# The first load as two halves of 64 partitions, one issued by SyncE and one by ScalarE

## The chip, the core and the metric

The kernel runs on one core of a Trainium2 chip. A core has TensorE (PE; its weight loads are listed apart as PEld), VectorE (DVE), ScalarE (ACT), GpSimd (POOL) and SyncE (SP), and 16 DMA engines that move data between HBM and the on-chip buffer (SBUF, 128 partitions). DMAs are issued by an engine's instruction into that engine's queue: SyncE's is q1 in the profile, ScalarE's is q10. The metric is the device time of one execution in microseconds; a profiled execution also gives a trace, whose span runs from the first to the last instruction.

## The reference

One token attends to two cached attention blocks, A with 16 heads and B with 16 query heads over 8 key heads. The two results are mixed by a gate.

```python
q = (x @ wq).reshape(B, Sq, H, Dh).transpose(0, 2, 1, 3)          # 448 -> 16 x 256
p = softmax(einsum("bhqd,bhkd->bhqk", q, k_cache) * Dh ** -0.5)   # over 8192 keys
a = einsum("bhqk,bhkd->bhqd", p, v_cache) -> (1, 1, 4096) @ wo    # the same for b, with k, v
                                                                  # repeated for two heads each
g = sigmoid((x * gate_w).sum(-1, keepdims=True))
return g * a + (1 - g) * b
```

Keys and values of A (16 heads) and of B (8 heads) are 8192 x 256 float32 each: 24 heads x 2 x 8.39 MB. With the weights, 432 MB are read once and 448 numbers are written.

## The kernel before

All inputs are laid out ahead of time as one long array, `stream`, in the order in which the kernel wants them. `plan()` (line 42) lists the pieces: the token and gate weights ("xg"), the query weights of a step ("wq"), tiles of keys ("k") and of values ("v", three tiles behind their keys), the output weights ("wo"). There are 8 steps; each has three units of work (a pair of B's heads that share keys, and two heads of A), each unit four tiles of 2048 keys. The pieces are packed into loads of up to `FULL` = 15872 floats per partition (62 KB, 7936 KB over 128 partitions). The first load holds 15368 floats per partition: "xg", the first "wq", two tiles of keys and most of a third.

The loads go into a ring of three buffers of SBUF, the tile named `slot`. The loop at line 629 walks over the list: it takes the next buffer, issues the load with `nc.sync.dma_start` on SyncE's queue, and then calls `piece()` for every piece in it, which issues the work on it. `Recorder.call` (line 147) tracks which instruction reads or writes what, and puts a wait on a semaphore where an engine or a DMA has to wait for another; every DMA has a semaphore of its own (dma0, dma1, ...). The instructions all appear at line 183 of the profile, where the recorder issues them, so tiles tell them apart. A load into a buffer waits until all that read its former content is done. So SyncE issues three loads at once at the start, and each later one when its buffer comes free.

On the first load, VectorE copies the token into `xz` (function `inputs`), TensorE multiplies it with the query weights (`project`), ScalarE and TensorE turn and spread the query (`spread`), and then the scores of the first keys follow: TensorE multiplies into `ps_sc`, VectorE takes minima (`mn`), ScalarE the exponential (`px`), VectorE turns it (`pr`). For one unit per step ("by row") VectorE multiplies the keys in the buffer itself and sums (`slot<-slot,qa`, `sr<-slot`). Values are multiplied on TensorE into `ps_o`. ScalarE issues one DMA in the whole kernel, at its end: half of the output. SyncE issues the other half.

```python
    for fill in LOADS:
        buf = ring.tile([P, FULL], F32, name="slot")
        c = 0
        for load in fill:
            n = sum(x[3] for x in load)
            nc.sync.dma_start(buf[:, c:c + n], stream[off:off + P * n].rearrange("(p n) -> p n", p=P))
```

Of the kernel before, what the change touches and what calls it, by code (L numbers as in the profile page):

```python
# [9 lines left out]
P = 128  # L10
# [214 lines left out]
def program(nc, stream, out):  # L225
    nc.alloc_sbuf_tensor("pad", [P, -((nc.sbuf_base + 31) // 32 * 32) % 256 // 4 or 64], F32)
    memory = {("slot", i): nc.alloc_sbuf_tensor(f"slot_{i}", [P, FULL], F32) for i in range(SLOTS)}
    plan = Recorder(nc, memory)
    build(plan, stream, out)
    names = ["tensor", "vector", "scalar", "gpsimd"] + plan.dmas  # L230
    sems = {n: nc.alloc_semaphore(f"{n[0]}{n[1]}" if n[0] == "dma" else n) for n in names}
    rec = Recorder(nc, memory, plan.needed | {(e, plan.count[e] - 1) for e in names[:4]}, sems)
    stores = build(rec, stream, out)
    late = rec.wait("sync", [(e, rec.count[e] - 1) for e in names[:4]] + [d for d in rec.dmas if d not in stores[1:]])
    for sem, value in late:
        nc.sync.wait_ge(sem, value)
    nc.sync.sem_clear(range(sems[names[0]].num, sems[stores[1]].num))
    for d in stores[1:]:
        nc.sync.wait_ge(sems[d], 16)
    nc.sync.sem_clear(range(sems[stores[1]].num, sems[stores[-1]].num + 1))  # L240


def build(nc, stream, out):
# [335 lines left out]
    def piece(kind, i, at, view):  # L579
        n = view.shape[-1] // ATOM[kind]  # L580
        j0 = at // ATOM[kind]
        if kind == "xg":
            inputs(view[:, :KF + 1])
            GW[0] = view[:, KF + 1:]
        elif kind == "wq":
            project(i, j0, view.rearrange("p (c n) -> p c n", c=n))
            if j0 + n < 2 * KF + 1:
                pass
            elif i == 0:
                spread(0)  # L590
                prepare(GW[0])
            else:
                wait(1, spread, i)
        elif kind == "k":
            u, t = TILES[i]
            if u in BY_ROW:
                scores_by_row(u, t, 2 * j0, view.rearrange("p (j d) -> p j d", d=DH))
            else:
                scores(u, t, j0, view.rearrange("p (c n) -> p c n", c=n))
            if j0 + n < 2 * NG:  # L600
                return
            tick()
            if t == NT - 1:
                gather(u)
                wait(1, combine, u)
                wait(2, column, u)
        elif kind == "v":
            u, t = TILES[i]
            n = view.shape[-1] // DH
            attend(u, t, at // DH, n, view.rearrange("p (j d) -> p j d", d=DH))  # L610
            if at // DH + n == ROWS:
                if t == NT - 1:
                    take(u)
                    if u != TILES[-1][0]:
                        wait(1, project_o, u)
                if i >= len(TILES) - LEAD:
                    tick()
        elif kind == "half":
            emit_half(i, view)
        elif kind == "wo" and i < NS - 1:  # L620
            emit_set(i, j0, view.rearrange("p (c n) -> p c n", c=n))
            if i == NS - 2 and j0 + n == 8:
                fold()
        else:
            for j in range(n):
                LAST[divmod(j0 + j, 2)] = view[:, j * D:(j + 1) * D]

    off = 0
    for fill in LOADS:
        buf = ring.tile([P, FULL], F32, name="slot")  # L630
        c = 0
        for load in fill:
            n = sum(x[3] for x in load)
            nc.sync.dma_start(buf[:, c:c + n], stream[off:off + P * n].rearrange("(p n) -> p n", p=P))
            off += P * n
            for x in load:
                piece(*x[:3], buf[:, c:c + x[3]])
                c += x[3]
# [71 lines left out]
```

## Time and profile before

| | |
|---|---|
| median of 3 runs | 1007.69 us (1007.64 to 1007.72) |
| profiled execution | 1007.64 us |
| its span | 1006.0 us |
| mean granted TensorE clock | 0.771 |
| read from HBM | 432.02 MB |
| loads by SyncE | 64, of which 50 of 7936 KB and the first of 7684 KB |

The page gives busy time by engine, the span in 40 slices (25.15 us each), the DMA queues, the chain of work that ended last, and groups of instructions with the idle time ahead of them and what ended it. The issue rows of the trace give the time from issue to landing of a DMA. The table of windows gives, for any stretch, each engine's busy time and the packets that the DMA engines started in it, as a share of 16 engines and in GB/s; in stretches shorter than a packet the share can exceed 1, since a packet counts in full where it starts. Queues called "instruction" (q8, q14) fetch program code.

### The profile page before, as it was taken

How to read it: one execution, taken by the hardware profiler on the slowest of the kernel's cores; microseconds unless marked ns; L12 is line 12 of the kernel's file. 1: busy time of each engine (PE TensorE's matmuls, PEld its weight loads, DVE VectorE, ACT ScalarE, POOL GpSimd, SP SyncE). 2: the span in 40 equal slices, each digit the busy share in tenths (PEclk: the TensorE clock that was granted, in tenths of full speed). 3: DMA queues.
4: the chain of work that ended last, by engine and by line, in shares of the span. 5: the costliest groups of instructions: out<-in, count | busy, mean ns of one | idle time of the engine just before them, and what ended most of it. 6: DMA issues, size and time to landing. Idle time of an engine off the chain costs nothing.

```text
span 1006.0 us, 7381 instructions
## 1 busy us (share of the span) xinstructions
PE 577.4 (57%) x3154; PEld 168.9 (17%) x3154; DVE 458.5 (46%) x642; ACT 94.5 (9%) x308; POOL 1.9 (0%) x10
## 2 busy tenths in 40 slices
PE   1846746654645665646736565545555647536557
PEld 0212211121111111112211121111111112111112
DVE  1386213961248521566214851248521585115951
ACT  0100100010100110001100011100110101101011
POOL 0000000000000000000000000000000000000000
PEclk9977787777786787787877777776777877777779
DMA  9999999999999999999999999999999999999997
GB/s 394 443 442 432 420 440 440 434 422 437 440 432 429 430 442 432 432 432 440 428 434 435 439 423 435 442 435 422 435 442 437 422 432 442 438 427 425 442 419 332
DMA packets 9256, 432.48 MB, mean 430 GB/s; under 512 B 1032, under 2 KB 1288, under 8 KB 1928
## 3 DMA queue, kind: packets, MB, share of 16 engines
q1 hardware_dynamic: 9220, 432.02, 99.3%
q8 instruction: 24, 0.39, 0.1%
q14 instruction: 8, 0.07, 0.0%
q10 hardware_dynamic: 4, 0.00, 0.0%
HBM read 432.02 MB, written 0.00 MB: 429 GB/s over the span
## 4 chain that ended last, share of the span: by engine, by line
DMA 75%; DVE 12%; PE 11%; ACT 1%; issue 0%; SPq 0%
DMA slot<-in_stream_dram 75%; PE ps_o L183 5%; DVE sr L183 5%; DVE slot L183 5%; PE ps_sc L183 5%; PE ps_s L183 1%; DVE pr L183 1%; DVE mn L183 1%; ACT px L183 1%; ACT ew L183 0%; ACT pxr L183 0%; DVE st L183 0%; PE ps_y L183 0%; DVE wr L183 0%; DVE mt L183 0%
## 5 line engine op out<-in xcount | busy, mean ns | idle before, releaser
L183 PE MATMUL ps_o<-slot,pr 128*32 128x512 f32 (+1 forms) x1536 | 346.6, 752 | 241.3 <-DMA slot<-in_stream_dram 241.1
L183 PE MATMUL ps_sc<-slot,qb 128*32 128x512 f32 x1024 | 194.4, 713 | 97.9 <-DMA slot<-in_stream_dram 97.8
L183 DVE TENSOR_REDUCE mn<-ps_sc 128x1 f32<-128x512 f32 x64 | 44.1, 689 | 310.4 <-PE ps_sc L183 281.9
L183 DVE TENSOR_TENSOR slot<-slot,qa 128x4096 f32<-128x4096 f32 (+7 forms) x39 | 142.4, 3652 | 45.5 <-DMA slot<-in_stream_dram 45.5
L183 PEld LDWEIGHTS ps_o<-slot,pr 128*32 128x32 f32 (+1 forms) x1536 | 79.1, 141 | 421.0 <-DMA slot<-in_stream_dram 272.5
L183 DVE TENSOR_REDUCE sr<-slot 128x16 f32<-128x4096 f32 (+7 forms) x39 | 142.5, 3654 | 1.3
L183 PEld LDWEIGHTS ps_sc<-slot,qb 128*32 128x32 f32 x1024 | 46.2, 129 | 215.7 <-DMA slot<-in_stream_dram 113.1
L183 ACT ACTIVATE px<-ps_sc,st 128x512 f32<-128x512 f32 x64 | 44.0, 688 | 377.7 <-DVE st L183 377.7
L183 DVE STREAM_TRANSPOSE pr<-px 128x512 f32<-128x512 f32 x64 | 45.7, 714 | 54.2 <-ACT px L183 54.2
L183 PE MATMUL ps_s<-slot,xz 128*32 128x512 f32 (+1 forms) x136 | 46.3, 656 | 36.2 <-DVE xz L183 22.1
L183 ACT ACTIVATE pxr<-sr,st 128x16 f32<-128x16 f32 x32 | 9.9, 308 | 376.5 <-DVE st L183 376.5
L183 DVE SCALAR_TENSOR_TENSOR ob<-ps_o,half,ob 128x256 f32<-128x256 f32 x24 | 11.4, 475 | 69.3 <-ACT ob L183 69.3
L183 PE MATMUL ps_s<-sel,ob 128*128 128x1 f32 (+1 forms) x96 | 17.0, 281 | 25.1 <-DVE ob L183 25.1
L183 PEld LDWEIGHTS ps_s<-sel,ob 128*128 128x128 f32 x96 | 15.0, 221 | 48.4 <-DVE ob L183 42.2
L183 PEld LDWEIGHTS ps_s<-slot,xz 128*32 128x32 f32 (+1 forms) x136 | 11.6, 122 | 66.6 <-issue 28.6
L183 DVE TENSOR_TENSOR pr<-pxr,cols 128x256 f32<-128x256 f32 x32 | 13.6, 425 | 15.0 <-ACT pxr L183 15.0
L183 ACT ACTIVATE ob<-ps_o,half 128x256 f32<-128x256 f32 x24 | 11.3, 471 | 67.0 <-PE ps_o L183 66.9
L183 PE MATMUL ps_y<-slot,ocs 128*1 128x448 f32 (+1 forms) x176 | 16.7, 497 | 0.0
L183 PE MATMUL ps_s<-ones,wr 1*128 1x1 f32 x48 | 9.9, 273 | 11.6 <-DVE wr L183 11.6
L183 PE MATMUL ps_s<-px,spread 64*128 64x256 f32 x16 | 7.2, 537 | 12.7 <-DVE es L183 12.7
L183 PEld LDWEIGHTS ps_s<-ones,wr 1*128 1x128 f32 x48 | 7.8, 204 | 34.5 <-DVE wr L183 20.2
L183 ACT ACTIVATION_READ_ACCUMULATOR px<-ps_sc,st 128x1 f32 x64 | 12.4, 193 | 0.0
(62 smaller groups left out, 138.9 us busy)
## 6 DMA issues: line engine op xcount, KB each, us to landing
slot<-in_stream_dram SPq DMA_DIRECT2D x50, 7936.0 KB, 42.1
slot<-in_stream_dram SPq DMA_DIRECT2D x1, 7684.0 KB, 21.1
slot<-in_stream_dram SPq DMA_DIRECT2D x1, 4608.0 KB, 40.2
slot<-in_stream_dram SPq DMA_DIRECT2D x2, 2048.0 KB, 33.9
slot<-in_stream_dram SPq DMA_DIRECT2D x1, 3328.0 KB, 38.4
slot<-in_stream_dram SPq DMA_DIRECT2D x1, 1536.0 KB, 32.2
slot<-in_stream_dram SPq DMA_DIRECT2D x3, 448.0 KB, 33.3
slot<-in_stream_dram SPq DMA_DIRECT2D x1, 1024.0 KB, 32.6
```

What stands on the lines that cost most here:

```text
L183: i = getattr(e, what)(*args, **kw)
```

## The change

Only the load at the start of `stream` (`off == 0`) differs. Its rows are divided: partitions 0 to 63 are loaded by a DMA of SyncE, partitions 64 to 127 by a DMA of ScalarE, into the same columns of the same buffer. All other loads stay on SyncE's queue.

```diff
             n = sum(x[3] for x in load)
-            nc.sync.dma_start(buf[:, c:c + n], stream[off:off + P * n].rearrange("(p n) -> p n", p=P))
+            rows = stream[off:off + P * n].rearrange("(p n) -> p n", p=P)
+            if off == 0:
+                nc.sync.dma_start(buf[:P // 2, c:c + n], rows[:P // 2])
+                nc.scalar.dma_start(buf[P // 2:, c:c + n], rows[P // 2:])
+            else:
+                nc.sync.dma_start(buf[:, c:c + n], rows)
             off += P * n
```

On ScalarE, at the start of the program, these are the first instructions before (`px`, `qa` and `ge` belong to the query and the gate, `px,st` to the exponentials of the first scores):

```order
L183 ACT_TABLE_LOAD
L183 ACTIVATE px<-ps_s 64x512
L183 ACTIVATE qa<-ps_s 128x256
L183 ACTIVATE ge<-ps_s 1x1
L183 ACTIVATE px,st<-ps_sc,st 128x512 x4
L183 ACTIVATE pxr,st<-sr,st 128x16
```

and these with the change:

```order
L183 DMA slot<-in_stream_dram 64x15368
L183 ACT_TABLE_LOAD
L183 ACTIVATE px<-ps_s 64x512
L183 ACTIVATE qa<-ps_s 128x256
L183 ACTIVATE ge<-ps_s 1x1
L183 ACTIVATE px,st<-ps_sc,st 128x512 x4
```

The issue of the second half stands first on ScalarE, ahead of the load of its function table; the rest keeps its order. On VectorE, a piece of the difference at the place where the token is first read (`xz` is its tile; the names in brackets are the semaphores waited for):

```order
 L183 MEMSET qb_0 128x128 x4
 L183 MEMSET xz 128x160
-L183 COPY xz<-slot 128x3 [waits dma0,vector]
+L183 COPY xz<-slot 128x3 [waits dma0,dma1,vector]
 L183 COPY xz<-slot 64x1 x2
 L183 TENSOR_SCALAR qb_0<-ps_s 128x2x2 [waits tensor]
```

The copy waits for both halves. The loads after the first have numbers one higher, and on SyncE the first row covers 64 partitions instead of 128; nothing else moves on any engine.

## The prediction

> **What bounds the kernel now.** I read the page's first three parts, then the chain of waits, then SyncE's own waits, then the table of windows over the start.
>
> ```profile
> span 1006.0 us, 7381 instructions
> PE 577.4 (57%) x3154; PEld 168.9 (17%) x3154; DVE 458.5 (46%) x642; ACT 94.5 (9%) x308; POOL 1.9 (0%) x10
> DMA  9999999999999999999999999999999999999997
> GB/s 394 443 442 432 420 440 440 434 422 437 440 432 429 430 442 432 432 432 440 428 434 435 439 423 435 442 435 422 435 442 437 422 432 442 438 427 425 442 419 332
> q1 hardware_dynamic: 9220, 432.02, 99.3%
> q10 hardware_dynamic: 4, 0.00, 0.0%
> DMA 75%; DVE 12%; PE 11%; ACT 1%; issue 0%; SPq 0%
> ```
>
> No engine is busy more than 57% of the span, while packets of queue q1 (SyncE's loads) fill 99.3% of what 16 DMA engines could do. The rate is flat from the second slice to the last but one. The chain calls 75% DMA; its DVE and PE parts are the work that frees a buffer before the next load is issued. Whether that ever starves the queue is seen here:
>
> ```profile
> DMA to landing us min/median/max: 21.1/40.6/58.7
> slot<-in_stream_dram SPq DMA_DIRECT2D x1, 7684.0 KB, 21.1
> slot<-in_stream_dram SPq DMA_DIRECT2D x2, 7936.0 KB, 49.0
> 0.74 0.39 SPq L183
> 1.20 39.29 DMA slot<-in_stream_dram
> 1.65 0.43 SPq L183 DMA_DIRECT2D slot<-in_stream_dram  x1
> 37.12 0.33 SPq L183 DMA_DIRECT2D slot<-in_stream_dram  x1
> 21.90 0.40 DVE L183 COPY xz<-slot 128x3 f32<-128x3 f32 x3 [15.88 <-DMA slot<-in_stream_dram]
> ```
>
> A full load is 128 x 15872 x 4 bytes = 8.13 MB, 18.9 us at 430 GB/s. The median load lands 40.6 us after its issue, more than two such times: when one is issued, over a load is still ahead of it in the ring. So the kernel is one stream of 432 MB that never runs dry, and the end comes when the stream ends. An edit at the start is worth exactly what it does to the stream's bytes per microsecond there. That the first data come earlier or later to the engines costs nothing by itself. The first load is issued at 0.74 and lands at 21.84 us (VectorE uses it at 21.90). The fourth load, which reuses its buffer, is issued at 37.12, 15.3 us after that landing. The second, issued at 1.20, lands 39.29 us later; with a mean of 49.0 for the two 7936 KB loads of the start, the third, issued at 1.65, lands 58.7 us later, the longest of all, at about 60.3, so 23 us of stream stand ahead of the fourth. The first load may land up to 23 us later, with the others in place, before the ring empties.
>
> **The start, packet by packet.** The columns are window, length, busy time of PE, PEld, DVE, ACT and POOL, granted clock, DMA share, GB/s. A packet is counted where it starts, so share x 16 x length / count is the mean time of one.
>
> ```profile
> 1.70:1.80 0.10, 0.00 (x0) 0.00 (x0) 0.10 (x2) 0.10 (x1) 0.10 (x1) 1.00 6.09 1844
> 2.40:2.50 0.10, 0.00 (x0) 0.00 (x0) 0.07 (x2) 0.00 (x0) 0.00 (x0) 1.00 1.98 615
> 2.50:2.60 0.10, 0.00 (x0) 0.00 (x0) 0.10 (x2) 0.00 (x0) 0.00 (x0) 1.00 0.00 0
> 4.90:5.00 0.10, 0.00 (x0) 0.00 (x0) 0.04 (x1) 0.00 (x0) 0.00 (x0) 1.00 5.67 2459
> 253.00:253.10 0.10, 0.10 (x5) 0.09 (x9) 0.10 (x1) 0.00 (x0) 0.00 (x0) 1.00 1.46 635
> ```
>
> One row of the first load is 15368 x 4 = 61,472 bytes, and 1844 GB/s x 0.1 us is three of them: one packet is one partition's row, 128 packets in all, 8 for each of 16 engines. All 16 engines start between 1.7 and 2.5 us, and nothing starts in the next window. The first packets take 6.09 x 16 x 0.1 / 3 = 3.25 us. In the second round four packets take 5.67 x 16 x 0.1 / 4 = **2.27 us** each: 27.1 GB/s per engine. In mid-kernel a 63,488-byte row takes 1.46 x 16 x 0.1 = 2.34 us, again 27.1. Sixteen times 27.1 is 434, the flat rate of the page. So each packet moves at a fixed 27.1 GB/s, and the engines start their rounds in step.
>
> **The change, part by part.** SyncE's half and ScalarE's half carry the same 7.87 MB as before, 64 packets each, 4 per engine, if each half is spread over 16 engines as every load here is.
>
> *Issue.* ScalarE gets one issue ahead of its table load.
>
> ```profile
> 0.73 1.28 ACT L183 ACT_TABLE_LOAD   x1 [0.73 <-PEq L697]
> 28.77 0.59 ACT L183 ACTIVATE px<-ps_s 64x512 f32<-64x512 f32 x1 [26.75 <-PE ps_s L183]
> 1003.77 1.10 ACTq L183 DMA_DIRECT2D out_dram<-ys  x1
> ```
>
> The only issue of ScalarE in the trace took 1.10 us, so the table load slips by about that, to end near 3.1 us; ScalarE's first work was at 28.77, behind 26.75 us of idle time. Cost 0; the idle time covers it. SyncE's issue stays first in its queue. VectorE's first COPY waits for two semaphores where it waited for one, and those queued behind it on VectorE (the query's setup, then the first score reductions) come with it; priced by the 23 us of slack above: 0.
>
> *The two rings on one engine.* New is that each of the 16 engines has packets of two queues at once. The nearest rows are the instruction fetches (q8, q14) that meet the loads. Ahead of each row stands the window in which the packet starts, then the queue's packets, MB and share of 16 engines.
>
> ```profile
> 254.80:254.90 0.10, 0.10 (x8) 0.09 (x4) 0.10 (x1) 0.00 (x0) 0.00 (x0) 1.00 3.48 1434
> q8 instruction: 1, 0.02, 110.1%
> 255.70:255.80 0.10, 0.10 (x8) 0.05 (x4) 0.00 (x0) 0.00 (x0) 0.00 (x0) 1.00 1.81 635
> q1 hardware_dynamic: 1, 0.06, 361.5%
> ```
>
> The q8 packet starts at 254.85 and takes 110.1% x 16 x 0.05 us = 0.88 us; a load packet starts at 255.75, just as it ends, and takes 361.5% x 16 x 0.05 = 2.89 us where 2.34 is usual. So an engine changes queue between packets, not inside one, and the load's packet behind a change is 0.55 us longer. For the first load that is up to 8 such changes on each engine: between 0 (both rings have their packets ready) and 8 x 0.55 = 4.4 us.
>
> *Where the packets of a round go.* Before, the 16 packets of a round are spread over the 128 rows of the buffer. Now the engines, in step, take a round from SyncE's ring and then one from ScalarE's. All 16 packets of a round lie in partitions 0-63, and of the next in 64-127. Whether the 27.1 GB/s is what an engine can move, or what the stretch of buffer it writes can take, no row tells, since no load of this kernel covers less than 128 partitions. If it is the engine, a round still takes 2.27 us: 0. If it is the destination, twice as many engines share each and a round takes 4.54 us: 8 x 2.27 = **+18.2 us** on the first load. Two engines that share a destination and started apart by d each have it alone for d in every round. The starts spread over 0 to 0.7 us; I take 0.3, which gives back 8 x 0.3 = 2.4. [...]
>
> [...]
>
> *Sum.* I take the destination: 18.2 - 2.4 = +15.8 us. The profiled execution took 1007.64 (span 1006.0 and 1.64 around it), 0.05 under the median of 1007.69. Forecast 1007.64 + 15.8 = **1023.4 us**. Bounds of this case: 18.2 - 8 x 0.7 = +12.6 (1020.2) and 18.2 + 4.4 = +22.6 (1030.2). None of it is won back later, since the ring behind it is never dry: the first load would land near 37.6, the fourth be issued 15.3 us later at 53, and the third, shifted as well, land near 76.
>
> **The rivals.**
> - *Queue changes alone.* The engine is the limit, but each alternation costs what the fetch rows show. 7 changes x 0.55 = 3.9 us gives 1011.5; between half and all eight of them, 1009.8 to 1012.0. For: measured here on load packets. Against: a fetch comes alone and unannounced, while ScalarE's ring has its four packets ready beside SyncE's.
> - *No change: the same 16 engines, the same bytes.* It decides if 27.1 GB/s is the engine's and a waiting ring is ready at once: every packet still 2.27 us, 1007.6, with at most the 0.9 us by which the first packets exceed the second, either way: 1006.7 to 1008.6. For: nothing in the trace moves slower when more or fewer packets start together. Against: the 0.55 us row. [...]
> - *Faster.* Two issuers would fill 16 engines sooner. The whole stretch from the first issue at 0.74 to the last engine's start at 2.5 is 1.8 us, under 0.2% (2.0 us, about what a measurement of this kernel can tell from no change).
> - *The change doesn't do what it says.* The order of instructions shows ScalarE's issue first on its engine, ahead of the table load, with the same release as SyncE's. If its half came a packet late it would land 2.27 us later among the second load's packets, at the same total: the no-change case.
>
> **How the numbers follow.** Engine or destination is open by the trace, so I give each half. The destination reading needs the engines in step as well, and the starts show that: **0.50** for the forecast. The other half splits between queue changes alone (**0.25**), no change (**0.23**) and faster (**0.02**). Slower by over 0.2% are the first two, less a sliver where only few changes cost: 0.74; within 0.2%: 0.24; faster 0.02. The forecast's own range is 1020.2 to 1030.2. To leave out no more than 2 in 10 the range must take in the no-change case too: 1007.2 to 1027.5, which leaves out the top of the forecast's own range, where all eight queue changes would cost in full, and the bottom of the no-change case.
>
> **What would show it.** In the changed profile queue q10 should hold some 64 large packets, 3.9 MB. Forecast: packets of both queues in the first 38 us take about 4.2 to 4.5 us, the first slice of GB/s falls from 394 to some 200 to 250, VectorE's COPY starts near 37 and the fourth issue comes near 53; from there all rows read as before, some 16 us later. Queue changes alone: packets of 2.8 us, COPY near 26. No change: packets of 2.27 us, COPY at 22. I am wrong if the first load's packets keep 2.27 us, or if lost time at the start is won back by the end, which would mean that the stream was not the bound.

## The result and the profile after

The changed kernel takes 1025.89 us (median; 1025.82 to 1026.13), beside 1007.72 us (1007.64 to 1007.91) for the kernel before in the same series: a ratio of 1.018 (1.0169 to 1.0191), 18.2 us slower. One run of the first try with two loads, further down, fell in a slower state (1066.94 us) and is left out of the figures there. From the page of the changed kernel, the span, the DMA slices (25.6 us each) and the queues:

```profile
span 1024.5 us, 7382 instructions
DMA  9999999999999999999999999999999999999998
GB/s 223 310 425 429 432 434 434 434 431 434 435 434 434 436 432 434 434 436 434 434 432 429 434 432 434 434 435 436 434 434 436 432 431 434 435 436 432 436 410 335
q1 hardware_dynamic: 9156, 428.09, 97.5%
q10 hardware_dynamic: 84, 3.94, 1.8%
DMA 73%; PE 13%; DVE 11%; ACT 1%; issue 0%; another core or an unknown queue 0%; SPq 0%; DVEq 0%
```

Nearly the whole loss is in the first two slices: 223 and 310 GB/s where before stood 394 and 443; from the third on (425 and up) the rate is about the old one. The DMA share stays at nine tenths or more all the while. The DMA engines are not idle at the start; their packets take longer. The timeline gives the issues and the first use of the load:

```profile
0.74 0.61 ACTq L183 DMA_DIRECT2D slot<-in_stream_dram  x1
1.37 1.28 ACT L183 ACT_TABLE_LOAD   x1 [1.37 <-PEq L702]
41.18 0.40 DVE L183 COPY xz<-slot 128x3 f32<-128x3 f32 x3 [35.17 <-DMA slot<-in_stream_dram]
56.47 0.33 SPq L183 DMA_DIRECT2D slot<-in_stream_dram  x1
```

VectorE's first COPY moved from 21.90 to 41.18 us, and the fourth load's issue follows 15.3 us later, as before. The DMA queues in the windows 6 to 7 us (first line) and 11 to 12 us (second), with packets, MB and their time as a share of 16 engines:

```profile
q10 hardware_dynamic: 11, 0.68, 317.0%
q1 hardware_dynamic: 12, 0.74, 345.5%
```

A packet of ScalarE's half takes 317.0% x 16 us / 11 = 4.61 us, one of SyncE's half 345.5% x 16 / 12 = 4.61 us, instead of 2.27. Between 2.0 and 40 us there are eight rounds of 16 packets, and the windows show the queues taking turns. 8 x (4.61 - 2.27) = 18.7 us stands beside a difference of the spans of 18.5. That close an agreement is partly chance. The first round took 4.45 us, and before it had taken 3.1 and not 2.27, so the eight rounds are worth 1.35 + 7 x 2.34 = 17.7 us. The rest is a start that came 0.4 us later and a first round of the second load that took 2.8 us instead of 2.35.

### The profile page after: what moved, and what is told of

The parts are those of the page before. It is cut to its first block, busy times and chain, and to the rows that moved or that the text cites. A ratio compares the mean times of both kernels' runs of the same rounds, so it can differ in the third digit from the quotient of the medians.

```text
span 1024.5 us, 7382 instructions
## 1 busy us (share of the span) xinstructions
PE 576.6 (56%) x3154; PEld 169.0 (17%) x3154; DVE 458.9 (45%) x642; ACT 94.4 (9%) x308; POOL 1.9 (0%) x10
## 4 chain that ended last, share of the span: by engine, by line
DMA 73%; PE 13%; DVE 11%; ACT 1%; issue 0%; another core or an unknown queue 0%; SPq 0%; DVEq 0%
DMA slot<-in_stream_dram 73%; PE ps_o L183 6%; PE ps_sc L183 5%; DVE sr L183 4%; DVE slot L183 4%; PE ps_s L183 2%; DVE pr L183 1%; ACT px L183 1%; DVE mn L183 1%; PE ps_y L183 0%; ACT ew L183 0%; DVE st L183 0%; DVE wr L183 0%; ACT pxr L183 0%
## 5 line engine op out<-in xcount | busy, mean ns | idle before, releaser
L183 PE MATMUL ps_sc<-slot,qb 128*32 128x512 f32 x1024 | 198.0, 728 | 95.0 <-DMA slot<-in_stream_dram 94.9
L183 PE MATMUL ps_s<-sel,ob 128*128 128x1 f32 (+1 forms) x96 | 16.7, 278 | 26.7 <-DVE ob L183 26.7
L183 PE MATMUL ps_y<-slot,ocs 128*1 128x448 f32 (+1 forms) x176 | 14.6, 447 | 0.0
L183 PEld LDWEIGHTS ps_s<-ones,wr 1*128 1x128 f32 x48 | 7.4, 193 | 30.9 <-DVE wr L183 17.7
```

The source lines that it names most:

```text
L183: i = getattr(e, what)(*args, **kw)
```

## The experiments

All differ from the changed kernel in the issue of the first one or two loads only; of each diff the lines that say how are shown. The packets that a queue has for one DMA engine are called its ring there. D is the theory that the written part of the buffer sets the rate, Q that two rings on an engine cost the time, L that the late landing of the first load does.

**Both halves on SyncE.**

```diff
-                nc.scalar.dma_start(buf[P // 2:, c:c + n], rows[P // 2:])
+                nc.sync.dma_start(buf[P // 2:, c:c + n], rows[P // 2:])
```

> Both 64-partition halves of the first load are issued by SyncE, one behind the other; ScalarE issues none. Theory D (the part of the buffer that a round of packets goes to is the limit: in a round all 16 packets lie in one half, so each takes twice as long): packets of the first load 4.5 to 4.6 us again, VectorE's first COPY near 41, 1025 to 1027 us. Rival Q (two rings on one engine cost the time): packets of 2.27 us, COPY near 22, 1007.5 to 1008.5 us.

Measured: 1027.24 us, ratio 1.0193 (1.0177 to 1.0208). Queue q1 from 6 to 7 us:

```profile
q1 hardware_dynamic: 12, 0.74, 361.2%
```

That is 4.82 us a packet, with no second ring, a little above the 4.5 to 4.6 that was expected (as the time is above 1025 to 1027). ScalarE's part in the change is not what costs; Q falls.

**Two queues, all partitions each.**

```diff
+                nc.sync.dma_start(buf[:, c:c + n // 2], rows[:, :n // 2])
+                nc.scalar.dma_start(buf[:, c + n // 2:c + n], rows[:, n // 2:])
```

> The first load is divided by columns, not by partitions: SyncE and ScalarE each load half of the columns of all 128 partitions. Theory D: rows of 30.7 KB, 16 packets per engine at 1.13 us, 18.2 us for the load as before, 1007.5 to 1008.5 us. Rival Q: a change of queue at every packet; with the 0.55 us that a load packet took longer behind a fetch, 16 x 0.55 = 8.8 us, 1016 us; with the doubling of the changed kernel, 1026 us.

Measured: 1007.54 us, ratio 0.9997 (0.9988 to 1.0007). The queues from 9 to 10 us:

```profile
q1 hardware_dynamic: 14, 0.43, 99.7%
q10 hardware_dynamic: 2, 0.06, 14.2%
```

Rows of 30.7 KB take 99.7% x 16 / 14 = 1.14 us, 27 GB/s for each engine, though the queues take turns: from 10 to 11 us 13 packets of q10 start beside 2 of q1. The changes between the two rings cost nothing here that can be measured (1007.54 us beside 1007.67 for the kernel before in the same series); the 0.55 us behind an instruction fetch does not carry over to them.

**Smaller neighbourhoods**, all on SyncE: four DMAs of 32 partitions, and eight of 16.

```diff
+                for q in range(0, P, 32):
+                    nc.sync.dma_start(buf[q:q + 32, c:c + n], rows[q:q + 32])
```

> Four DMAs of 32 partitions each (0-31, 32-63, 64-95, 96-127), all by SyncE. Theory D leaves open how partitions share destinations. If evenly by neighbourhood, a quarter has a quarter of the rate: packets of 9.1 us, 8 x (9.1 - 2.27) = +54.6 us, 1062 us. If a quarter reaches as much as the half it lies in: 4.6 us, 1026 us. Rival Q: 1007.7 us. [...]

> Eight DMAs of 16 partitions each, all by SyncE, one packet per engine and DMA. Theory D: packets at least twice as long as those of the run with 32 partitions if 16 partitions reach half as much as 32: 9.1 us and 1062 us if those took 4.6; 18.2 us and 8 x (18.2 - 2.27) = +127 us, 1135 us, if those took 9.1. If 16 reach as much as 32, the time of that run again. Rival Q: 1007.7 us.

Measured: 1026.97 us (ratio 1.0189, 1.0172 to 1.0206) with 32 partitions and 1058.45 us (1.0502, 1.0481 to 1.0523) with 16. Queue q1 with 32 partitions, from 6 to 7 us:

```profile
q1 hardware_dynamic: 12, 0.74, 361.4%
```

and with 16, from 36 to 37 us, where ten of the 20 packets are rows of 61 KB and ten are of under 512 B:

```profile
q1 hardware_dynamic: 20, 0.61, 550.1%
```

Seven packets of under 512 B take 0.8% x 16 / 7 = 0.02 us each in the run with 8 rows out of step below (queue q1, 14 to 15 us), so a row takes (550.1% x 16 - 10 x 0.02) / 10 = 8.8 us with 16 partitions. It is 4.82 us with 32, just as with 64. So DMAs into 32 neighbours moved as fast as into 64, and those into 16 little more than half as fast. With 32 that is the case that was put at 4.6 us and 1026, with 16 the one at 9.1 us and 1062.

**Even and odd partitions.**

```diff
+                nc.sync.dma_start(buf[0::2, c:c + n], rows[0::2])
+                nc.scalar.dma_start(buf[1::2, c:c + n], rows[1::2])
```

> Again 64 rows for SyncE and 64 for ScalarE, but the even partitions for one and the odd ones for the other, so that each half covers the whole buffer. If what counts is how much of the buffer a half reaches: packets of 2.3 us, 1007.5 to 1008.5 us. If any 64-row DMA loses half the rate, or rows that share a destination still meet in a round: 4.6 us, 1026 us. If ScalarE's part in it matters: 1026 us too.

Measured: 1007.87 us, ratio 1.0002 (0.9992 to 1.0011). `Recorder.call` takes the two interleaved halves for overlapping and makes ScalarE's wait, so it was issued only at 13.4 us, after SyncE's had landed. SyncE's half alone, from 9 to 10 us:

```profile
q1 hardware_dynamic: 10, 0.61, 141.8%
```

2.27 us a packet: 64 rows at full rate, with no other half beside them. Neither the number of rows nor the missing partner is the cost; that the rows are neighbours is (4.61 us a packet in the changed kernel).

**Which side of the transfer.** The two loads are issued as four halves, the first spread where it is written and together where it is read, the second the other way round (`second` is the second load's part of the stream, `early[1]` its buffer).

```diff
+                nc.sync.dma_start(buf[0::2, c:c + n], rows[:P // 2])
+                nc.sync.dma_start(early[1][:P // 2, :m], second[0::2])
+                nc.scalar.dma_start(buf[1::2, c:c + n], rows[P // 2:])
+                nc.scalar.dma_start(early[1][P // 2:, :m], second[1::2])
```

> One side of the transfer at a time. The first load's halves are read as rows 0-63 and 64-127 of the stream, but written to the even and the odd partitions. The second load's halves are read as even and odd rows, but written to partitions 0-63 and 64-127. So both loads put their rows into other partitions than the reference wants. If the written side sets the rate (theory D): packets of the first load 2.27 us, of the second 4.6 to 4.8 us. If the side that is read sets it: the first 4.6, the second 2.34. If neither alone does: all near 2.3, 1008 to 1010 us; if each does: all 4.6 to 4.8, 1043 to 1046 us. Total for either side alone: 1024 to 1029 us.

Measured: 1035.13 us (two runs, 1032.81 and 1037.45). As in the run before, ScalarE's issues waited, until 13.27 us. The queues from 9 to 10 us (the first load's even half), from 16 to 17 us (the second load's first half) and from 21 to 22 us (the first load's odd half, in turns with the second load's):

```profile
q1 hardware_dynamic: 13, 0.80, 184.3%
q1 hardware_dynamic: 11, 0.70, 341.8%
q10 hardware_dynamic: 11, 0.68, 223.7%
```

Read as neighbours but written apart: 184.3% x 16 / 13 = 2.27 us. Read apart but written as neighbours: 4.97 us. The written side set the rate, as D has it. The total came out above the 1024 to 1029 that was expected for one side alone. The third line is a place where time went that D's sum had not counted: packets that are written apart took 3.25 us instead of 2.27 while other engines still worked on neighbouring rows. Over the four rounds of that half it makes about 2.4 us; the rest of the excess is not explained, and the two runs lie 4.6 us apart.

**Late landing.** The second load, whole, on ScalarE, so that it alternates with the first. In a first try its issue stood where the loop has it:

```diff
+            first = off == P * sum(x[3] for x in LOADS[0][0])
+            (nc.scalar if first else nc.sync).dma_start(buf[:, c:c + n], rows)
```

> The first load stays whole on SyncE; the second load, whole too (128 partitions), is issued by ScalarE at the start, so that the two alternate on every engine and the first lands at about twice its time. Theory D with the slack of 23 us: packets of 2.3 us, VectorE's first COPY near 38 to 40, as late as with the change, but a total of 1007.5 to 1009.5 us. Rival L (the loss comes from the late landing of the first load, not from the stream's rate): 1022 to 1026 us. Rival Q (each change of ring costs 0.55 us): 16 x 0.55 = +8.8, 1016.5 us.

Measured: 1031.31 us, ratio 1.0238 (1.0222 to 1.0253): a miss, and not by L, since the first COPY started at 22.01 us. The issue was queued behind ScalarE's work on the first load, the second load's first packets started only at 39 us, and the stream ran dry, as the table of windows shows (columns as in the prediction):

```profile
60.00:78.00 18.00, 0.00 (x0) 0.00 (x0) 0.00 (x0) 0.00 (x0) 0.00 (x0) 0.50 0.93 402
78.00:95.00 17.00, 11.53 (x52) 3.09 (x52) 12.08 (x11) 1.56 (x4) 0.00 (x0) 0.88 0.01 1
```

For 17 us nothing was loaded, and after 116 us the queue was dry once more, for about 2.5 us. With the issue ahead of ScalarE's first work (`second` and `early[1]` as above):

```diff
+                nc.sync.dma_start(buf[:, c:c + n], rows)
+                nc.scalar.dma_start(early[1][:, :m], second)
```

> As e5_late_landing, but ScalarE's issue of the whole second load stands at the very start of its program, ahead of its first work, which e5 had not done. Both loads cover 128 partitions and alternate on every engine. Theory D with the slack of 23 us: packets of 2.3 us, first COPY near 37 to 39, fourth issue near 53, total 1007.5 to 1010 us. Rival L (the late landing of the first load is what costs): 1023 to 1026 us.

Measured: 1008.38 us (1007.75 to 1010.18), ratio 1.0008 (0.9998 to 1.0017). Queue q1 from 7 to 8 us and q10 from 9 to 10 us, then VectorE's first COPY:

```profile
q1 hardware_dynamic: 15, 0.92, 212.8%
q10 hardware_dynamic: 14, 0.89, 204.9%
```

```profile
40.68 0.40 DVE L183 COPY xz<-slot 128x3 f32<-128x3 f32 x3 [34.67 <-DMA slot<-in_stream_dram]
```

Packets of 2.27 and 2.34 us, a first use as late as in the changed kernel (40.68 beside 41.18), and no loss clear of the noise. L falls. In the even and odd run, too, the COPY came late, at 38.44, and cost nothing.

**Two loads in halves.** Again a first try left the second load's issue in the loop, behind ScalarE's work:

```diff
-            if off == 0:
+            if off <= P * sum(x[3] for x in LOADS[0][0]):
```

> The first and the second load are both divided into halves of 64 partitions, SyncE and ScalarE. Theory D: the cost doubles, 8 x (4.61 - 2.27) + 8 x (4.76 - 2.34) = 38 us, 1044 to 1047 us. Rival: a cost of the start of ScalarE's queue that is paid once: 1026 us.

Measured: 1047.74 us (up to 1049.6; ratio 1.0402, 1.0385 to 1.042), above the range. The second load's half on ScalarE was issued at 55.24 us, behind ScalarE's work on the first load, and started only at 61 us, in turns with the third load, whole. Queue q1 from 73 to 74 us, the whole load's packets, which take 113.8% x 16 / 6 = 3.03 us beside that half:

```profile
q1 hardware_dynamic: 6, 0.38, 113.8%
```

With all four issues at the start:

```diff
+                for t, r in ((buf[:, c:c + n], rows), (early[1][:, :m], second)):
+                    nc.sync.dma_start(t[:P // 2], r[:P // 2])
+                    nc.scalar.dma_start(t[P // 2:], r[P // 2:])
```

> First and second load both divided into 64-partition halves, all four issues at the very start, ahead of ScalarE's first work. Theory D: 16 rounds of about 4.6 to 4.7 us, no other delay: 2 x 18.2 = +36.4, 1043 to 1046 us. Rival (paid once at the start of ScalarE's queue): 1026 us.

Measured: 1045.06 us, ratio 1.037 (1.0355 to 1.0385). The cost was paid by each of the loads so divided: +37.4 us for two, +18.2 for one.

**Out of step.** An extra DMA ahead of SyncE's half delays 8 engines, or one, by a short packet.

```diff
+                idle = nc.memory["slot", 2].ap()
+                nc.sync.dma_start(idle[64:96:4, :6912], rows[64:96:4, :6912])
```

> As the changed kernel, but ahead of its half SyncE loads 8 rows of 27.6 KB (0.2 MB that nothing reads) into the third buffer, which should occupy 8 of the 16 engines for about 1 us, so that those 8 then take ScalarE's half first, out of step with the other 8. Theory D in step: where two engines that share a destination are out of step, each has it alone part of the time; with a lead of 1.27 of 2.27 us a packet takes about 2.27 + 1.0 = 3.3 us instead of 4.6, COPY near 30, 1013 to 1019 us. If the engines that share a destination are both among the 8, or step doesn't matter: 1026 to 1028 us.

> As e7_out_of_step, but the extra DMA has one row of 27.6 KB, so that one engine alone is put out of step. If two engines share a destination and meet there because they are in step: in each round of the first load two of the 16 packets are shorter (2.4 to 4 us), the other 14 stay at 4.6. If many engines share one limit, or step doesn't matter: all 16 stay at 4.6. Total 1025 to 1029 us either way, since the slowest engines set the landing.

Measured: 1028.96 us (ratio 1.0209, 1.0192 to 1.0226) with 8 rows, 1026.52 us (1.0187, 1.0166 to 1.0207) with one. The first is above both ranges that were expected, and far from the 1013 to 1019 that shorter packets would have given. Its queue q1 from 12 to 13 us and q10 from 14 to 15 us:

```profile
q1 hardware_dynamic: 6, 0.37, 177.2%
q10 hardware_dynamic: 7, 0.43, 209.8%
```

Eight packets start on partitions 0-63 between 12.0 and 13.3 us, and eight on 64-127 between 13.7 and 15 us. They take 4.73 and 4.80 us, so from 13.3 to 16.7 us eight engines were at work on each half, and no faster for it than sixteen on one. Queue q1 of the run with one row, from 8 to 9 us and from 11 to 12 us:

```profile
q1 hardware_dynamic: 1, 0.06, 29.0%
q1 hardware_dynamic: 11, 0.68, 316.7%
```

In the first line one engine is on SyncE's half (partitions 0-63) by itself from 8.0 to 11.0 us; fifteen packets of ScalarE's half had started between 6 and 8 us and last to 11 and beyond. Its packet still takes 29.0% x 16 = 4.64 us, as long as each of the 11 that follow together. So the loss does not need engines that meet on a half in step.

## Why the prediction was right, and where its sum was off

- **The bound held.** One stream that never runs dry, so that only bytes per microsecond count: all slices after the second are about as before, a late landing alone cost nothing clear of the noise (1008.38 us), and where the queues did run dry, for 17 us and then 2.5, the end moved by 23.5.
- **The issue cost nothing.** ScalarE's issue took 0.61 us, the table load ended at 2.65, and ScalarE's first work waited for data as before.
- **Engine or destination.** The prediction gave each half the weight and took the destination. The run with one side at a time shows it: 2.27 us where rows are written apart, 4.97 where they are written as neighbours.
- **The size.** Forecast +15.8, measured +18.2. The step that failed is the 2.4 us taken back for engines that start apart: the first round's starts lay between 2.0 and 3.3 us, and no packet was shorter for it. With that term at 0 the sum is 18.2. The measured 4.61 us a packet instead of 4.54 adds 8 x 0.07 = 0.6. The sum also took the first round as one of 2.27 us before, though the prediction's own lines show 3.25 for its first packets; that takes 1.0 back. The late start and the slower first round of the second load add 0.9.
- **In step.** The doubling to 4.54 us was worked out from this: engines in step, so that twice as many share a destination at once. Both runs out of step speak against that form of it (4.64 us for an engine alone on its half, 4.73 and 4.80 for eight on each). That the doubling still gave nearly the right size is to that extent luck. What is shown is that the DMAs into 64 neighbouring partitions ran at half the rate (13.3 GB/s an engine instead of 27.1), and that the written side decided (4.97 us a packet written as neighbours, 2.27 written apart). Why stays open. A rival that no run tests is the dealing of rows to engines: a half by neighbours may give an engine other rows than a whole load does, where columns or even partitions need not, and no view here names the engine of a packet.
- **Queue changes at 0** was the author's choice in the sum. No run shows that term by itself between two halves; what the runs showed is 1.14 us a packet and no loss by columns, where the queues take turns as well, and 4.82 us a packet with both halves on one queue beside 4.61 with two. The rival that priced the changes at 3.9 us fell with the run by columns (1007.54 us). **No change** fell because 27.1 GB/s is not what an engine moves wherever it writes: the same 16 engines gave 13.3 each.
- **What was to be seen.** Packets forecast at 4.2 to 4.5 us: 4.61. First slice forecast at 200 to 250 GB/s: 223. COPY near 37: 41.18. Fourth issue near 53: 56.47.

## What to carry to other kernels

Where one stream of loads is the bound, ask of an edit only what it does to the stream's rate: a load whose first use came 19 us later (40.68 us beside 21.90) cost nothing that shows with the ring behind it full (1008.38 us), and one that moved at half rate (4.61 us a packet instead of 2.27) cost its full 18 us. If a load has to be divided over two queues, divide it by columns (1007.54 us) or by even and odd partitions (1007.87, where the two halves did not run at the same time), not into neighbouring partitions (1025.89). Put the issue of a DMA on a compute engine's queue ahead of that engine's work in the program: in the first tries with two loads ScalarE's issue waited behind its work (until 55.24 us with halves), and with the whole second load the stream ran dry for 17 us (1031.31 us beside 1008.38 with the issue ahead).

## What the runs showed of the hardware beyond that

A packet of a divided load was slower when only one queue was at work (4.82 us with both halves on SyncE) than with two in turns (4.61). Packets written over the whole buffer took longer while other engines worked on a half of neighbours: 3.25 us instead of 2.27, and 3.03 instead of 2.34 in the first try with two loads. And neither an engine alone on its half (4.64 us) nor eight on each (4.73 and 4.80) were faster for it. No further run went into these three.
